# Attention and a two-layer ReLU network in one kernel: from unit 3 on q and k are split for two heads at once, scores run as 64-row float16 matmuls, V is split once per unit, g's low parts go to VectorE, and a unit's first layer-2 block stands later

## The chip, the cores and the metric

The kernel runs on one core of a Trainium2 chip. The metric is the device time of one execution in microseconds (us); less is better.

## The reference, cut

```
scores = scale * np.matmul(q, k.transpose(0, 1, 3, 2))       # q, k, v: batch 4, 8 heads, 768 positions, 64 columns
is_global = pos[None, :] < n_global                          # 8
is_local = (rel >= 0) & (rel < n_local)                      # 96
scores = scores - slopes[:, None, None] * dist[None, :, :]   # -1e9 where neither holds
a = np.exp(scores - max); a = a / (sum + 1e-09)
x = np.matmul(a, v)                                          # as 3072 tokens of 512 columns
h = x @ w_in                                                 # w_in 512 x 2048, float32
g = np.maximum(h, 0.0) + alpha * np.minimum(h, 0.0)
out = g @ w_out                                              # w_out 2048 x 512, float32
```

## The kernel before

The 3072 tokens are cut into 12 units of 256 (three to a batch). A query sees at most 96 keys back and 8 global ones, so a unit needs four 128-key blocks of K and V (three in units 0, 3, 6 and 9, which begin a batch). Each unit goes through attention, head by head (`attend`), and then through the network: 16 blocks of layer 1 (`ff_in`, 12 matmuls of 256 columns into a PSUM tile `h`) and 16 of layer 2 (`ff_out`, for each of two 128-token halves 3 matmuls of 512 columns into an accumulator `o`). float32 accuracy is kept with pairs of float16 numbers: a high part, and a rest that `rest` works out; a product is then the three matmuls high by high, high by low, low by high.

Units 0 to 2 are "plain": their scores and values are float32 matmuls (the scores on 64 rows, `sp<-first` and `sp<-raw`), and their probabilities are transposed on TensorE. From unit 3 on one head goes like this. One DMA brings q and k (each twice, on partitions 0 to 63 and again on 64 to 127) and V as `raw` (464 KB, 368 KB in units 3, 6, 9). ScalarE or VectorE scales q into `q2` and k into `khi` (L343, L344), VectorE writes the rests (L368): q's into the lower 64 partitions of `q2`, k's into `klo`. The scores `sp` are then two 128-row matmuls a window, `q2` by `khi` and `q2` by `klo` (L656). V is split in the same way into `vhi` and `vlo`. VectorE adds the bias and finds the maximum (L662), ScalarE takes the exponential (L667), the result is split into `ps`, a DMA transposes it into `pt`, and 18 or 24 matmuls for two heads make `av` (L733), which VectorE scales into `xn`. After eight heads `xn` is split and transposed by DMA into `xt`, the input of layer 1. Behind layer 1 ScalarE multiplies by alpha, VectorE takes the maximum (`g`, L816), ScalarE makes the high part (L818), and VectorE or GpSimd the low one (L367).

The order on every engine comes from a planner (`Plan`): each operation has a key (its due time in slots of one `ff_in` and one `ff_out`), engines it may run on with a cost each, and buffers; the planner plays the program through and the instructions are then issued in the order that it found. `begin(u)` is the slot at which unit u's attention begins: 22 slots before its first `ff_in`, so that units' attention runs beside the network of the unit before. Numbers of buffers: `sp` 2, `av` 2, `h` 2, `o` 2 in PSUM; `raw` 2, `khi`, `klo`, `q2` 2, `vhi`, `vlo` 3, and 17 buffers `rw` of 4 KB a partition, which hold raw weights early and `g` later. Unit 1's accumulators are, by `ff_out`, one `sp` and one `av` buffer; every other unit uses the two `o`.

## Time and profile before

| | |
|---|---|
| time, median of 3 runs | 657.1 us (656.23 to 658.21) |
| the profiled execution's own time | 655.59 us |
| its span, first to last instruction | 653.8 us |
| TensorE (PE) busy | 624.0 us, 95% |
| VectorE (DVE) busy | 518.0 us, 79% |
| ScalarE (ACT) busy | 406.8 us, 62% |
| GpSimd (POOL) busy | 129.1 us, 20% |

In the rows, an instruction stands as line, engine, operation, out<-in with buffer numbers left out, the shape, and a count; the share of time that an engine sat idle before a group stands behind it with the engine and line that ended it. A matmul's busy time runs to the modelled end of its pipeline, so that matmuls which follow each other overlap; what one costs is read from start to start.

### The profile page before, as it was taken

The page shows a single profiled execution, that of the slowest core. Times are in us where ns is not written, and L with a number is a line of the kernel's source. Part 1 is how long each engine was busy: PE and PEld are TensorE (multiplying, and loading weights), DVE is VectorE, ACT ScalarE, POOL GpSimd, SP SyncE. Part 2 cuts the span into 40 slices and gives each one's busy share as a digit, 9 for nine tenths or more (in the row PEclk, how much of TensorE's full clock was granted, in tenths as well). Part 3 has the DMA queues.
Part 4 walks back from the last instruction along what each step waited for, and adds up shares of the span by engine and source line. Part 5 has one row for each costly group of instructions (what it writes and reads, how often), then busy time and mean ns, then how long its engine had stood idle before and what let it go on. Part 6 is the DMA issues. An engine that isn't in the chain of part 4 may idle for free.

```text
span 653.8 us, 13833 instructions
## 1 busy us (share of the span) xinstructions
PE 624.0 (95%) x4964; PEld 438.0 (67%) x4964; DVE 518.0 (79%) x1497; ACT 406.8 (62%) x1085; POOL 129.1 (20%) x185
## 2 busy tenths in 40 slices
PE   8998998999999999899899999999899999999995
PEld 7785666675666666576567676676576677676663
DVE  6899999868888899877989887877988888874331
ACT  6998866536756666766666665673656666653332
POOL 1003342212222223112222122111222112100000
PEclk9999999999999999999999999999999999999998
DMA  8998311115747546843656647764666646621001
GB/s 307 403 406 330 102 59 60 59 55 152 179 103 172 148 105 129 236 116 92 136 151 139 188 102 126 204 155 63 171 156 124 172 133 125 167 47 38 33 1 39
DMA packets 115807, 92.90 MB, mean 142 GB/s; under 512 B 93968, under 2 KB 93968, under 8 KB 115728
## 3 DMA queue, kind: packets, MB, share of 16 engines
q1 hardware_dynamic: 115728, 91.91, 52.1%
q8 instruction: 41, 0.67, 0.4%
q14 instruction: 38, 0.31, 0.2%
HBM read 63.06 MB, written 6.29 MB: 106 GB/s over the span
## 4 chain that ended last, share of the span: by engine, by line
PE 33%; DVE 30%; DMA 20%; ACT 11%; issue 4%; POOL 1%; SPq 0%; ACTq 0%; DVEq 0%; POOLq 0%
DMA raw<-in_qkv_dram 15%; PE o L835 13%; PE h L795 13%; ACT pr L667 4%; DVE ps L368 4%; DVE g L816 3%; DVE klo L368 3%; PE sp L656 3%; DVE q L368 2%; DVE vlo L368 2%; PE av L733 2%; DMA xt<-xs 2%; DMA vr<-in_v_dram 2%; DVE pr L662 2%; DVE vhi L344 2%
## 5 line engine op out<-in xcount | busy, mean ns | idle before, releaser
L795 PE MATMUL h<-xt,whl 128*128 128x256 f16 x2304 | 281.2, 273 | 1.6 <-DVE g L816 1.2
L795 PEld LDWEIGHTS <-whl 128*128 128x128 f16 x2304 | 224.6, 98 | 63.4 <-issue 3.0
L835 PE MATMUL o<-whl,g 128*128 128x512 f16 x864 | 215.6, 379 | 5.4 <-ACT os L842 5.3
L835 PEld LDWEIGHTS <-g 128*128 128x128 f16 x864 | 82.6, 98 | 71.6 <-issue 8.1
L367 POOL TENSOR_TENSOR g<-g 128x256 f16<-128x256 f32 x88 | 67.9, 773 | 256.5 <-ACT g L818 254.1
L667 ACT ACTIVATE pr<-pr,sm 128x256 f32<-128x256 f32 (+1 forms) x192 | 92.7, 484 | 34.9 <-DVE sm L662 34.5
L343 ACT ACTIVATE g<-h,ak 128x256 f32<-128x256 f32 x167 | 77.9, 467 | 55.2 <-PE h L795 52.6
L816 DVE SCALAR_TENSOR_TENSOR g<-h,g 128x256 f32<-128x256 f32 x192 | 80.0, 418 | 32.4 <-ACT g L343 32.0
L818 ACT CAST g<-g 128x256 f16<-128x256 f32 x144 | 57.1, 399 | 59.0 <-DVE g L816 58.6
L662 DVE CUSTOM_DVE_ANT_0 pr<-sp,D 128x256 f32<-128x256 f32 (+1 forms) x192 | 71.3, 393 | 3.5 <-PE sp L656 2.7
L368 DVE SCALAR_TENSOR_TENSOR ps<-pr,ps 128x512 f16<-128x512 f32 (+1 forms) x72 | 49.0, 680 | 12.9 <-ACT ps L343 12.6
L835 PE MATMUL o<-whl,gh 128*128 128x512 f16 x192 | 57.2, 379 | 0.7 <-ACT gh L818 0.6
L367 POOL TENSOR_TENSOR gl<-g,gh 128x256 f16<-128x256 f32 x32 | 30.2, 945 | 110.2 <-ACT gh L818 99.2
L368 DVE SCALAR_TENSOR_TENSOR klo<-raw,khi 128x416 f16<-128x416 f32 (+1 forms) x72 | 43.6, 605 | 1.8
L835 PE MATMUL o<-whl,gl 128*128 128x512 f16 x96 | 36.5, 380 | 2.4 <-POOL gl L367 2.0
L368 DVE SCALAR_TENSOR_TENSOR q<-raw,q 64x256 f16<-64x256 f32 x72 | 32.8, 455 | 6.8 <-ACT q L343 3.9
L367 DVE TENSOR_TENSOR g<-g 128x256 f16<-128x256 f32 x56 | 23.8, 425 | 16.5 <-ACT g L818 16.3
L656 PE MATMUL sp<-klo,q 128*128 128x256 f16 (+1 forms) x144 | 34.0, 263 | 2.3 <-DVE klo L368 2.3
L667 ACT ACTIVATION_READ_ACCUMULATOR pr<-pr,sm 128x1 f32 x192 | 36.2, 189 | 0.0
L733 PEld LDWEIGHTS <-pt 128*128 128x128 f16 x792 | 28.4, 98 | 11.3 <-DMA pt<-ps 3.5
L368 DVE SCALAR_TENSOR_TENSOR vlo<-raw,vs,vhi 128x256 f16<-128x256 f32 (+1 forms) x72 | 35.8, 517 | 0.1
L656 PE MATMUL sp<-khi,q 128*128 128x256 f16 (+1 forms) x144 | 33.8, 264 | 2.1 <-DVE sm L662 1.3
(122 smaller groups left out, 734.6 us busy)
## 6 DMA issues: line engine op xcount, KB each, us to landing
raw<-in_qkv_dram SPq DMA_DIRECT2D x56, 464.0 KB, 3.9
w<-in_w_dram SPq DMA_DIRECT2D x32, 512.0 KB, 9.0
raw<-in_qkv_dram SPq DMA_DIRECT2D x24, 368.0 KB, 3.4
out_dram<-os SPq DMA_DIRECT2D x24, 256.0 KB, 2.4
vr<-in_v_dram SPq DMA_DIRECT2D x18, 256.0 KB, 4.0
first<-in_first_dram SPq DMA_DIRECT2D x4, 464.0 KB, 5.3
vr<-in_v_dram SPq DMA_DIRECT2D x3, 512.0 KB, 8.4
first<-in_first_dram SPq DMA_DIRECT2D x4, 336.0 KB, 10.1
```

Source lines behind the costliest of these rows:

```text
L343: lambda: nc.scalar.mul(out=out(), in_=src(), mul=by.t if tile_ else by)),
L344: DVE=("DVE", c_dve(n, not psum, tile_), lambda: v.tensor_scalar(out=out(), in0=src(), scalar1=by.t if tile_ else by, scalar2=None, op0=AL ...
L367: return e.tensor_tensor(out=out(), in0=src(), in1=hi(), op=ALU.subtract)
L368: return e.scalar_tensor_tensor(out=out(), in0=src(), scalar=val(), in1=hi(), op0=ALU.mult, op1=ALU.subtract)
L656: nc.tensor.matmul(sp.t[:, pc : pc + n], lhsT=q_()[:, 128 * qb : 128 * qb + 128], rhs=kk()[:, off : off + n], start=j == 0, stop=j == len( ...
L662: op("DVE", key, c_dve(n) + 10, lambda qb=qb, n=n, dc=dc, pc=pc: v.tensor_tensor_reduce(out=pr.t[:, pc : pc + n], in0=sp.t[:, pc : pc + n] ...
L667: op("ACT", key + 1, c_act(n, ptr=1) + 93, lambda qb=qb, n=n, pc=pc: nc.scalar.activation(out=pr.t[:, pc : pc + n], in_=pr.t[:, pc : pc + ...
L733: nc.tensor.matmul(out, lhsT=p_[:, 128 * j : 128 * j + 128], rhs=v_[:, 64 * j : 64 * j + 64], start=m == 0, stop=m == len(ps) - 1)
L795: nc.tensor.matmul(hp.t, lhsT=w.t[:, wi, wc], rhs=x.t[:, NC * xi + c, :], start=n == 0, stop=n == 3 * NC - 1)
L816: op("DVE", key, c_dve(UT), lambda: v.scalar_tensor_tensor(out=g_(), in0=hp.t, scalar=KG, in1=g_(), op0=ALU.mult, op1=ALU.max), r=[hp], w= ...
L818: op("ACT", key, c_act(UT), lambda: nc.scalar.copy(out=gh_(), in_=g_()), r=[rg], w=[rh])
L835: nc.tensor.matmul(o.t, lhsT=g_()[:, tok], rhs=w.t[:, wi, 512:1024], start=f == 0 and n == 0, stop=f == NF - 1 and n == 2)
```

## The change

From unit 3 on, `load_pair` takes the place of the splits of q and k: one DMA brings two heads' q and k, head 2i on partitions 0 to 63 and head 2i+1 on 64 to 127 (344 KB, 272 KB in units 3, 6, 9), one instruction makes the high parts `x16` of all of it and one the rests, and the scores of both heads are issued together: for each window three products, each for the one head and then the other, on 64 rows, into two `sp` buffers. `load_v` loads a unit's V once (512 KB), scales and splits it for all heads in four instructions, and builds the blocks of earlier and global keys `gp` by DMAs of up to 96 partitions from this and the last unit's tiles; the matmuls of `av` read `v16` and `gp`. Unit 2 loads q, k and V in the form of unit 1. g's low parts from unit 3 on name VectorE first instead of GpSimd. `ff_out` of block 0 is due at slot 4.05 behind its `ff_in` instead of 3, the others at 3.05. The V ranges of a batch (`v_range`) are due four slots earlier. The layouts in DRAM are made to match. Lines of the changed kernel are some 28 higher in `ff_in` and `ff_out` (L823, L863), scores stand at L648 and `av` at L761.

```
-BUFS = dict(rw=17, raw=2, q2=2, khi=2, klo=2, vhi=3, vlo=3, pr=2, sm=6, pt=2, ps=2, xn=1, xt=2, g=3, gh=3, gl=3,
+BUFS = dict(rw=17, raw=3, x16=3, pr=2, sm=6, pt=2, ps=2, xn=1, xt=2, g=3, gh=3, gl=3,
...
+            x = buf("rw", f"first{u}_{h}", [P, 1024]) if u < 2 else buf("raw", f"first{u}_{h}", [P, 672])
...
+        v16, gp = {}, {}
+        def load_v(u, key):
+            b, c = divmod(u, 3)
+            raw = buf("rw", f"vraw{u}", [P, 1024])
+            x = v16[u] = buf("rw", f"v16_{u}", [P, 1024])
+            g = gp[u] = buf("rw", f"gp{u}", [P, 1024])
+            view = lambda y: y.t.bitcast(F16).rearrange("p (j s k) -> p j s k", j=2, s=2)
+            op("SP", key, c_dma(P * 4096), lambda: nc.sync.dma_start(
+                out=raw.t.rearrange("p (j k) -> p j k", j=2), in_=a["v"][b, 2 * c : 2 * c + 2].rearrange("j p k -> p j k")),
+               w=[raw])
+            for j in range(2):
+                in_ = lambda j=j: raw.t[:, 512 * j : 512 * j + 512]
+                hi, lo = (lambda j=j: view(x)[:, j, 0]), (lambda j=j: view(x)[:, j, 1])
+                k = key + VS + 0.1 * j
+                mul(k, hi, in_, vs[b], [raw, vs[b]], [(x, (j, 0))], "ACT", 512)
+                rest(k, lo, in_, vs[b], hi, [raw, vs[b], (x, (j, 0))], [(x, (j, 1))], 512)
+            key += VS + 1
+            def move(i, part, to, first, last, src, j, parts):
+                n = last - first
+                op("SP", key + 0.1 * i, c_dma(n * 2048), lambda: nc.sync.dma_start(
+                    out=view(g)[to : to + n, i], in_=view(src)[first:last, j]), r=[(src, p) for p in parts], w=[(g, part)])
+            if c:
+                move(0, "0p", 0, GL, P, v16[u - 1], 1, ((1, 0), (1, 1)))
+                move(0, "0g", LOC, LOC, P, gp[u - 1], 1, ("1g",))
+                move(1, "1g", LOC, LOC, P, gp[u - 1], 1, ("1g",))
+            else:
+                move(1, "1g", LOC, 0, GL, x, 0, ((0, 0), (0, 1)))
+            move(1, "1p", 0, GL, P, x, 0, ((0, 0), (0, 1)))
+        def blocks(u):
+            own = [(v16[u], j, [(v16[u], (j, t)) for t in range(2)]) for j in range(2)]
+            far = [(gp[u], j, [(gp[u], f"{j}p"), (gp[u], f"{j}g")]) for j in range(2)]
+            return [far[0], own[0], far[1], own[1]] if u % 3 else [own[0], far[1], own[1]]
+        pair = {}
+        def load_pair(u, h, key):
+            nk = 416 if u % 3 else 288
+            n = 256 + nk
+            raw = buf("raw", f"raw{u}_{h}", [P, 672])
+            x = buf("x16", f"x16_{u}_{h}", [P, 2, 672], F16)
+            op("SP", key - KP - 4, c_dma(P * 4 * n), lambda: nc.sync.dma_start(
+                out=raw.t[:, :n], in_=a["qk"][u - 1, h // 2, :, :n]), w=[raw])
+            hi, lo = (lambda: x.t[:, 0, :n]), (lambda: x.t[:, 1, :n])
+            mul(key - KP, hi, lambda: raw.t[:, :n], QS, [raw], [(x, 0)], n=n)
+            rest(key - KP, lo, lambda: raw.t[:, :n], QS, hi, [raw, (x, 0)], [(x, 1)], n)
+            if (u, h) == (3, 0):
+                for i in range(H):
+                    op("POOL", key - KP, c_pool(384, 1), lambda i=i: nc.gpsimd.tensor_scalar(
+                        out=Dh[i].t, in0=Dh[i].t, scalar1=QS * QS, scalar2=None, op0=ALU.mult), w=[Dh[i]])
+            sps = [buf("sp", f"sp{u}_{h + i}", [P, 512]) for i in range(2)]
+            for i in range(2):
+                pair[u, h + i] = sps[i]
+            def scores():
+                for qb, off, m, _, pc in windows(u):
+                    for j, (qi, ki) in enumerate(((0, 0), (0, 1), (1, 0))):
+                        for i, sp in enumerate(sps):
+                            rows = slice(64 * i, 64 * i + 64)
+                            nc.tensor.matmul(sp.t[:, pc : pc + m], lhsT=x.t[rows, qi, 128 * qb : 128 * qb + 128],
+                                             rhs=x.t[rows, ki, 256 + off : 256 + off + m], start=j == 0, stop=j == 2)
+            op("PE", key, 3 * 0.426 * (512 if u % 3 else 384) + 300, scores, r=[x], w=sps)
         def attend(u, h, key):
...
-                raw = buf("raw", "raw" + uh, [P, 928])
-                op("SP", kp - 4, c_dma(P * 4 * (256 + nk + nv)), lambda: nc.sync.dma_start(
-                    out=raw.t[:, : 256 + nk + nv], in_=a["qkv"][u, :, h, : 256 + nk + nv]), w=[(raw, 0), (raw, 1)])
...
-                q2 = buf("q2", "q2_" + uh, [P, 256], F16)
-                q_ = lambda: q2.t
-                khi = buf("khi", "khi" + uh, [P, 416], F16)
-                klo = buf("klo", "klo" + uh, [P, 416], F16)
-                kk = lambda: rawt()[:, 256 : 256 + nk]
-                mul(kp, lambda: q2.t, lambda: rawt()[:, :256], QS, [rq], [q2], n=256)
-                mul(kp, lambda: khi.t[:, :nk], kk, QS, [rq], [khi], n=nk)
-                rest(kp, lambda: q2.t[64:, :], lambda: rawt()[64:, :256], QS, lambda: q2.t[64:, :], [rq], [q2], 256)
-                rest(kp, lambda: klo.t[:, :nk], kk, QS, lambda: khi.t[:, :nk], [rq, khi], [klo], nk)
...
-            if not plain:
-                vhi = buf("vhi", "vhi" + uh, [P, 256], F16)
-                vlo = buf("vlo", "vlo" + uh, [P, 256], F16)
-                vv = lambda: vrt()[:, :nv]
...
-                    mul(kp + 3, lambda: vhi.t[:, :nv], vv, vs[b], [rv, vs[b]], [vhi], "DVE", nv)
-                    rest(kp + 3, lambda: vlo.t[:, :nv], vv, vs[b], lambda: vhi.t[:, :nv], [rv, vs[b], vhi], [vlo], nv)
...
+                if h % 2 == 0:
+                    load_pair(u, h, key)
+                sp = pair[u, h]
...
-                    for j, (_, kk) in enumerate(keys):
-                        nc.tensor.matmul(sp.t[:, pc : pc + n], lhsT=q_()[:, 128 * qb : 128 * qb + 128],
-                                         rhs=kk()[:, off : off + n], start=j == 0, stop=j == len(keys) - 1)
-            op("PE", key, cost, scores, r=[q2] + [x for x, _ in keys], w=[sp])
+                    nc.tensor.matmul(sp.t[:, pc : pc + n], lhsT=qk_()[:, 128 * qb : 128 * qb + 128],
+                                     rhs=qk_()[:, 256 + off : 256 + off + n], start=True, stop=True)
+            if plain:
+                op("PE", key, 2 * npr * 0.84, scores, r=[q2], w=[sp])
...
+                vb = blocks(u)
+                def side(j, t):
+                    y, i, _ = vb[j]
+                    return y.t.bitcast(F16)[:, 1024 * i + 512 * t + 64 * h : 1024 * i + 512 * t + 64 * h + 64]
+                prods = lambda: ((pflat(), lambda j: side(j, 0)), (pflat(), lambda j: side(j, 1)),
+                                 (pflat()[:, npr:], lambda j: side(j, 0)))
+                used = [pt] + [x for _, _, y in vb for x in y]
...
-                        nc.tensor.matmul(out, lhsT=p_[:, 128 * j : 128 * j + 128], rhs=v_[:, 64 * j : 64 * j + 64],
+                        nc.tensor.matmul(out, lhsT=p_[:, 128 * j : 128 * j + 128], rhs=v_(j),
...
-            rest(key, gl_, g_, None, gh_, [rg, rh], [rl], UT, "DVE" if u < 2 and f < 2 else "POOL")
+            rest(key, gl_, g_, None, gh_, [rg, rh], [rl], UT, "DVE" if u > 2 or u < 2 and f < 2 else "POOL")
...
+            if u > 2:
+                jobs.append((begin(u) - VL, load_v, (u,)))
...
-                jobs.append((slot(u, f) + (DP if u < 2 else 1.5 if u == 2 else DL), ff_out, (u, f)))
+                jobs.append((slot(u, f) + (DP if u < 2 else 1.5 if u == 2 else DL + (1.05 if f == 0 else 0.05)), ff_out, (u, f)))
```

PE, the scores of unit 7's first two heads. Before: the last matmul of a layer-1 block `h5_10`, the weight load and the two products of head 0 (each stands twice, once a window), then layer 2; head 1 has the same rows later, behind `h5_12`.

```order
L795 MATMUL h5_10_4936<-xt5_4296,whl10_1349 128x256
L656 LDWEIGHTS q2_7_0_4864
L656 MATMUL sp7_0_4954<-khi7_0_4866,q2_7_0_4864 128x256
L656 MATMUL sp7_0_4954<-klo7_0_4894,q2_7_0_4864 128x256
L835 MATMUL o5_1_4593<-whl7_1097,g5_7_4812 128x512
```

Now:

```order
L823 MATMUL h5_10_4692<-xt5_4187,whl10_1356 128x256
L648 LDWEIGHTS x16_7_0_4226
L648 MATMUL sp7_0_4706<-x16_7_0_4226 128x256
L648 MATMUL sp7_1_4708<-x16_7_0_4226 128x256
L863 MATMUL o5_0_4478<-whl7_1089,g5_7_4605 128x512
```

The rows `sp7_0` and `sp7_1` stand six times each, turn about: two blocks of four matmuls have become one of twelve, and the second head's scores stand in the place of the first's.

PE where unit 5's layer 2 takes over the accumulators from unit 4 (`o4_1` with `g4_15` is unit 4's last block, `o5_0` with `g5_0` unit 5's first; one row for each block of 3, 4, 12 or 18 matmuls). Before:

```order
L656 MATMUL sp6_2_4534<-khi6_2_4501,q2_6_2_4499 128x256
L835 MATMUL o4_1_3857<-whl15_1732,g4_15_4398 128x512
L835 MATMUL o5_0_4552<-whl0_543,g5_0_4438 128x512
L656 MATMUL sp6_3_4561<-khi6_3_4527,q2_6_3_4525 128x256
L795 MATMUL h5_3_4570<-xt5_4296,whl3_812 128x256
L835 MATMUL o5_1_4593<-whl0_543,g5_0_4438 128x512
```

Now:

```order
L863 MATMUL o4_0_3754<-whl15_1737,g4_15_4266 128x512
L863 MATMUL o4_1_3772<-whl15_1737,g4_15_4266 128x512
L823 MATMUL h5_3_4413<-xt5_4187,whl3_802 128x256
L761 MATMUL av6_2_4433<-v16_6_4134,pt6_2_4314 128x64
L823 MATMUL h5_4_4458<-xt5_4187,whl4_858 128x256
L863 MATMUL o5_0_4478<-whl0_533,g5_0_4328 128x512
L863 MATMUL o5_0_4478<-whl1_594,g5_1_4356 128x512
```

Between the last block of the old unit and the first of the new stood nothing; now two layer-1 blocks and one of `av` stand there, and blocks 0 and 1 of layer 2 follow each other.

PE where unit 3's attention begins (`o1` is unit 1's accumulators, in an `sp` and an `av` buffer; rows as above, in part). Before, head 0 stood ahead of unit 1's last layer-1 block:

```order
L835 MATMUL o1_0_1010<-whl12_1485,gl1_12_1884 128x512
L656 MATMUL sp3_0_1996<-khi3_0_1976,q2_3_0_1974 128x128
L656 MATMUL sp3_0_1996<-klo3_0_1981,q2_3_0_1974 128x256
L835 MATMUL o1_0_1010<-whl13_1578,gl1_13_1956 128x512
L835 MATMUL o1_0_1010<-whl14_1639,gl1_14_2020 128x512
```

Now:

```order
L863 MATMUL o2_0_2139<-whl1_594,gl2_1_2136 128x512
L863 MATMUL o1_0_1000<-whl15_1737,gl1_15_2092 128x512
L648 MATMUL sp3_0_2179<-x16_3_0_1451 128x128
L648 MATMUL sp3_1_2181<-x16_3_0_1451 128x128
L648 MATMUL sp3_0_2179<-x16_3_0_1451 128x256
L648 MATMUL sp3_1_2181<-x16_3_0_1451 128x256
```

A pair takes both `sp` buffers, so unit 3's first scores stand behind the last block of `o1_0`; its four pairs then follow with some 1.5, 2 and 3.5 blocks of the network between them.

## Rows read from the trace of the kernel before

**Rows 1.** The page's first part: the span, then busy time, share of the span and instructions of each engine.

```profile
span 653.8 us, 13833 instructions
PE 624.0 (95%) x4964; PEld 438.0 (67%) x4964; DVE 518.0 (79%) x1497; ACT 406.8 (62%) x1085; POOL 129.1 (20%) x185
```

**Rows 2.** Busy time by stretch: the stretch in us, its length, then busy us and instructions of PE, PEld (weight loads), DVE, ACT, POOL, the granted clock of PE (1.00 is full speed), the share of the DMA engines and GB/s. 30 to 150 holds the network of units 0 and 1 and the splitting of the weights, 150 to 210 that of unit 2 beside unit 3's attention, 210 to 600 units 3 to 10, the last stretch unit 11 with no attention beside it.

```profile
30.00:150.00 120.00, 114.87 (x802) 82.95 (x803) 109.98 (x264) 84.50 (x205) 31.42 (x27) 1.00 0.45 159
150.00:210.00 60.00, 57.84 (x474) 38.35 (x473) 51.17 (x158) 39.43 (x106) 14.70 (x21) 1.00 0.60 145
210.00:600.00 390.00, 377.81 (x3208) 264.66 (x3206) 319.92 (x933) 242.32 (x664) 79.13 (x123) 1.00 0.57 137
600.00:653.80 53.80, 46.25 (x308) 30.03 (x305) 15.46 (x48) 17.00 (x37) 0.67 (x1) 0.96 0.06 22
```

**Rows 3.** Who waited for whom, 210 to 600 us: the matmuls (PE) and, last row, the weight loads. Columns: us in total, times, the longest.

```profile
PE o L835 <- ACT os L842: 5.3, 7, 2.2
PE av L733 <- DMA pt<-ps: 2.9, 5, 1.2
PE sp L656 <- DVE klo L368: 2.3, 8, 0.5
PE h L795 <- DVE g L816: 1.2, 2, 0.7
...
PEld L656 <- DVE q L368: 2.5, 7, 0.4
```

**Rows 4.** The same view, 140 to 210 us.

```profile
PE sp L656 <- DVE sm L662: 1.3, 2, 0.8
PE o L835 <- ACT gh L818: 0.6, 2, 0.4
...
PEld L835 <- POOL gl L367: 1.7, 3, 0.6
```

**Rows 5.** Instructions in order of time: start us, us, engine, line, operation, out<-in, shape, count, and in brackets the idle time before and what ended it. PE and ACT where unit 5's layer 2 begins.

```profile
261.93 0.81 PE L835 MATMUL o<-whl,g 128*128 128x512 f16 x3
...
264.23 0.67 ACT L842 ACTIVATE os<-o,osc 128x512 f32<-128x512 f32 x1
...
264.95 0.81 PE L835 MATMUL o<-whl,g 128*128 128x512 f16 x3 [2.21 <-ACT os L842]
```

**Rows 6.** PE in order of time: scores of unit 6 (128 and 256 columns), and blocks of both layers.

```profile
311.60 0.22 PE L656 MATMUL sp<-klo,q 128*128 128x128 f16 x1 [0.51 <-DVE klo L368]
311.66 0.27 PE L656 MATMUL sp<-khi,q 128*128 128x256 f16 x1
311.77 0.27 PE L656 MATMUL sp<-klo,q 128*128 128x256 f16 x1
...
313.94 1.47 PE L795 MATMUL h<-xt,whl 128*128 128x256 f16 x12
315.25 1.46 PE L835 MATMUL o<-whl,g 128*128 128x512 f16 x6
316.55 1.47 PE L795 MATMUL h<-xt,whl 128*128 128x256 f16 x12
318.07 0.23 PE L656 MATMUL sp<-khi,q 128*128 128x128 f16 x1
```

**Rows 7.** PE in order of time, unit 1's 64-row float32 scores: one head (21.52) and, later, two heads issued one behind the other on rows 0 to 63 and 64 to 127 (24.45), each with the block that follows.

```profile
21.52 1.13 PE L656 MATMUL sp<-first 64*128 64x256 f32 x4
22.58 0.66 PE L693 MATMUL tp<-ident,pr 128*128 128x128 f32 x4
...
24.45 1.14 PE L656 MATMUL sp<-first 64*128 64x256 f32 x8
25.52 1.09 PE L771 MATMUL xp<-ident,xn 128*128 128x128 f32 x8
```

**Rows 8.** PE in order of time: one such block of unit 2 between blocks of the network.

```profile
108.81 0.71 PE L795 MATMUL h<-xt,whl 128*128 128x256 f16 x5
109.45 1.13 PE L656 MATMUL sp<-raw 64*128 64x256 f32 x4
110.51 0.61 PE L835 MATMUL o<-whl,gh 128*128 128x512 f16 x2
```

**Rows 9.** Groups of equal instructions, shapes apart: count, busy us and mean ns of one, then idle time before them and what ended it.

```profile
L368 DVE SCALAR_TENSOR_TENSOR q<-raw,q 64x256 f16<-64x256 f32 x72 | 32.8, 455 | 6.8 <-ACT q L343 3.9
L368 DVE SCALAR_TENSOR_TENSOR klo<-raw,khi 128x416 f16<-128x416 f32 x48 | 31.9, 665 | 1.2
L368 DVE SCALAR_TENSOR_TENSOR vlo<-raw,vs,vhi 128x256 f16<-128x256 f32 x48 | 26.4, 571 | 0.1
L368 DVE SCALAR_TENSOR_TENSOR ps<-pr,ps 128x512 f16<-128x512 f32 x48 | 33.2, 692 | 12.7 <-ACT ps L343 12.6
L367 DVE TENSOR_TENSOR g<-g 128x256 f16<-128x256 f32 x56 | 23.8, 425 | 16.5 <-ACT g L818 16.3
L367 POOL TENSOR_TENSOR g<-g 128x256 f16<-128x256 f32 x88 | 67.9, 773 | 256.5 <-ACT g L818 254.1
L662 DVE CUSTOM_DVE_ANT_0 pr<-sp,D 128x256 f32<-128x256 f32 x160 | 64.8, 415 | 0.6 <-PE tp L693 0.3
```

**Rows 10.** DMA issues: tile, count, KB each, median us from issue to landing.

```profile
vr<-in_v_dram SPq DMA_DIRECT2D x18, 256.0 KB, 4.0
...
pt<-ps SPq DMA_TRANSPOSE x72, 3.1
```

More of the change, by code (lines that the diff above doesn't have):

```diff
@@ L315 @@
 WLEAD = 8
-VLEAD = 22
+VLEAD = 26.5
+VS = 5
+VL = 4
 WARM = 9
@@ L546, in load_first @@
         def load_first(u, h, key):
[L548 removed]
+            x = buf("rw", f"first{u}_{h}", [P, 1024]) if u < 2 else buf("raw", f"first{u}_{h}", [P, 672])
             nk, n = (672, 672) if u else (544, 928)
             def load():
[L552 removed]
+                nc.sync.dma_start(out=x.t[:, :n], in_=a["qk"][u - 1, h // 2] if u else a["first0"][h // 2])
                 if u == h == 0:
@@ L643, in attend @@
-            sp = buf(idle(u, h, "sp", "h"), "sp" + uh, [P, 512])
+                if u == 2 and h % 2 == 0:
+                    load_first(u, h, key - KP - 4)
+                q2, qk_ = first[u, h]
+                rv, vrt = firstv[u, h]
+                sp = buf(idle(u, h, "sp", "h"), "sp" + uh, [P, 512])
+            else:
+                if h % 2 == 0:
+                    load_pair(u, h, key)
+                sp = pair[u, h]
             pr = buf(idle(u, h, "pr", "stage"), "pr" + uh, [P, 512])
@@ L703, in attend @@
                 ps = buf("ps", "ps" + uh, [P, 2, 512], F16)
-                pt = buf("wf" if PT4 and u > 2 else "pt", "pt" + uh, [P, 2, 512], F16)
+                pt = buf("pt", "pt" + uh, [P, 2, 512], F16)
                 pp = lambda: pr.t[:, :npr]
```

72 lines of the change are left out of this document (15 added, 57 removed).

## Prediction

> **What bounds the kernel now.** I read the page's busy line first [rows 1]: TensorE is busy in 95% of the span, VectorE in 79%. A busy engine need not be the bound, so the table by stretch comes next [rows 2]: from 210 to 600 us TensorE works 377.8 of 390 us, at the granted clock 1.00 (the 2.4 GHz level), VectorE 319.9, ScalarE 242. So TensorE sets the time there, and a change can help in two ways only: fewer start-to-start nanoseconds of matmuls, or shorter waits of TensorE. In the last stretch, without attention beside it, there is nothing to win. From 30 to 150 us TensorE and VectorE are both near full (114.9 and 110.0 of 120), with weights to split, which the change leaves as it is.
>
> The floor of the matmuls, from start to start [rows 6]: a layer-1 block of 12 takes 1.31 us (0.109 each), a layer-2 block of 6 1.30, a score matmul of 256 columns 0.11 and of 128 columns 0.056.
>
> The waits are in the view of who waited for whom [rows 3]. Its idle time begins at a matmul's modelled end. In [rows 5] three matmuls start at 261.93, three times 0.216 later the next could start (262.58), and it starts at 264.95: 2.37 us lost where the row says 2.21. So I add 0.16 a wait. From 210 to 600 us:
> - layer 2's first block, for ScalarE to empty the accumulator (os): 5.3 + 7 x 0.16 = 6.4
> - av, for the transposes pt: 2.9 + 0.8 = 3.7
> - scores, for k's low part: 2.3 + 1.3 = 3.6; for q's, seen at the weight load, 318.07 against 316.55 + 1.31 [rows 6] is 0.21, I take 0.15 for each of 7, 1.0
> - layer 1, for g (a full h): 1.2 + 0.3 = 1.5
>
> Together 16.2 us. From 140 to 210 us [rows 4] the same count gives 1.3 + 0.6 + 0.6 for the matmuls' waits and 1.7 less some 0.2 each for those seen only at the weight loads, with q's about 4 us.
>
> **The change, part by part.**
>
> *Scores on TensorE.* Before: units 4, 5, 7, 8, 10, 11 have 8 heads x 4 matmuls x 0.109 = 3.5 us each, units 3, 6, 9 8 x 2 x (0.056 + 0.109) = 2.6 us; together 28.8 us. After: three products instead of two, each on half the rows. If two heads' matmuls on the two halves run at once, a pair costs 6 x 0.109 = 0.65 or 3 x 0.165 = 0.50 us, for 24 and 12 pairs 21.6 us; if they run one by one, 43.2. The trace decides for the first: one head's block of four 64-row matmuls takes 1.06 us to the next block's start (21.52 to 22.58), two heads' eight take 1.07 (24.45 to 25.52) [rows 7].
>
> But such a block costs something at its edges [rows 8]. From the start of five layer-1 matmuls at 108.81 to the layer-2 block at 110.51 pass 1.70 us; five by 0.109 and four float32 ones by 0.216 are 1.41. So 0.29 us go at each block for entering and leaving. The first weight load in it is a float32 one, longer than the float16 one here; bounds 0.20 and 0.30 us, I take 0.25, for 36 blocks 9.0 us (7.2 to 10.8). Net: 21.6 + 9.0 - 28.8 = +1.8 us (0 to +3.6). The saved matmuls pay for the edges, no more.
>
> The Trainium skill bears on both halves. TensorEngine Tiling (Array Packing), section Overview, gives a contraction of at most 64 rows "up to 2x"; by that alone the scores would give back 7.2 us and the sum below would end at 637. Its section Tiling Modes says that "Mode switching requires drain", without a price; the trace agrees, and prices it at 0.29 us a block.
>
> *Splits.* VectorE loses the rests of q (32.8 us), k (31.9, and those of units 3, 6, 9) and V (26.4, likewise) [rows 9], and scalings. It gains 36 rests of up to 672 columns (0.69 us at 512 columns, 0.665 at 416; 0.7 to 1.07 each: 25 to 39 us), 18 of V at 0.69 (12 us) and 88 low parts of g that were GpSimd's, at 0.425 (37 us): lighter by 10 us or more, with GpSimd's 67.9 us gone. None of this is on the path by itself, since TensorE is the bound. What it buys is that a split is ready in time. In order of issue the split of a pair now stands some 11 us of TensorE work ahead (x16 and raw have three buffers, each for two heads). So of 4.6 us for q and k I count 4.2 as gone.
>
> *Softmax and transposes.* Two heads' scores stand together; av stands, counted over the blocks between in the two orders, 16 us of TensorE work behind the scores instead of 9. The pt transposes take 3.1 us to land [rows 10]. Of 3.7 us I count 2.8 as gone. The price is a burst: four bias steps of 0.415 [rows 9] in a row ahead of g's next step. With VectorE lighter I count 0.8 of the 1.5 us for g as gone.
>
> *First layer-2 block.* Between a unit's last block and the next one's first stood 0 to 2.3 us of TensorE work; now two layer-1 blocks and an av block, 3.8 us from the first half's end. The longest wait was 2.37 us and the others 1.3 or less, so 5.8 of 6.4 us go.
>
> *Unit 3.* Unit 1's accumulator holds an sp buffer, so the first pair stands behind its last block, and the four pairs follow close. VectorE needs 4 x 0.3 to 0.4 us and the reads behind them, about 2 us, before sp is free, and the second pair stands 1.9 us behind the first. The waits of unit 2's g stay: its low parts remain GpSimd's. Bounds -2 and +3; I take +1.0.
>
> *V parts.* TensorE does the same matmuls. The DMAs that build gp are new; landing bounded by 0 and the 4.0 us of the V loads [rows 10], issued some 3 us behind a unit's first scores and needed 16 us behind them: hidden, 9 us to spare. Less DMA traffic is hidden either way (share 0.57 [rows 2]). Unit 2's new loads move the same scores: nothing.
>
> Sum, against the profiled execution's own 655.6: - 4.2 - 2.8 - 0.8 - 5.8 = -13.6, +1.8, +1.0: 644.8. That execution lies 1.5 us under the median of the runs, so 646.3; I say 646.
>
> **The rivals.**
>
> *All waits go and the edges are cheap.* 655.6 - 16.2 - 3 + 0 = 636.4, with the 1.5 638. For it: the waits are short and every cover grows. Against: unit 3's tight start.
>
> *The waits come back.* Bursts of a pair (four bias steps, four exponentials, the 672-column rest on VectorE ahead of g's maximum) make h or g late. If half of the 13.6 returns, 653. Against: layer 2 of a block stands three slots behind its layer 1, and some 6 us of TensorE work between a pair and the block that needs the delayed h.
>
> *The two heads don't overlap in float16.* 43.2 instead of 21.6 us: 644.8 + 21.6 + 1.5 = 668, slower. It decides once a pair's block costs 0.30 us more than forecast (the win of 10.8 us over 36 pairs); one by one it costs 0.60 more. Against it stands [rows 7], in float32.
>
> *V's parts late.* The gp DMAs stand in SP's queue behind V's last rest; should TensorE wait 2 us a unit, 18 us, 664: slower. From 1.2 us a unit the win is gone. Against: the 9 us to spare.
>
> **How the numbers follow.** Forecast (641 to 652) 0.62; all waits gone 0.13; waits back 0.13 (0.10 still faster, 0.03 within); no overlap 0.06; V late 0.06 (0.02 within). About 0.3% (2 us) is what a measurement of this kernel can tell from no change. Faster 0.85, same 0.05, slower 0.10. The range from 637 to 654 takes in the ends of the unknown costs and leaves out the two slow rivals and part of the first.
>
> **What would show it.** Right: per-pair blocks with two starts some 10 ns apart and about 0.65 us long plus 0.2 to 0.3 at the edges; os, klo and q gone from TensorE's waits or under 1.5 us together from 210 to 600 us; GpSimd nearly idle; VectorE under 510 us. Wrong: score matmuls of a pair 0.109 apart one by one; TensorE waiting for gp; new rows of h waiting for g of more than 5 us; or pairs waiting for sp beyond unit 3.

## The result, and the profile after

The kernel after takes 642.1 us (median of four runs, 638.8 to 642.4), the kernel before, beside it, 656.9: ratio 0.976, 95% interval 0.973 to 0.980. A second timing on another chip gave 0.973 (0.970 to 0.975). The forecast was 646 with a range of 637 to 654; faster had 0.85.

The profiled execution took 642.33 us, its span 640.5. The page's first part, as in [rows 1]:

```profile
span 640.5 us, 13718 instructions
PE 620.4 (97%) x5108; PEld 427.5 (67%) x5108; DVE 454.1 (71%) x1319; ACT 390.1 (61%) x1016; POOL 78.1 (12%) x108
```

Busy time by stretch, with the columns of [rows 2]:

```profile
30.00:150.00 120.00, 114.40 (x778) 82.48 (x776) 111.60 (x259) 83.77 (x200) 34.94 (x31) 0.97 0.47 165
150.00:210.00 60.00, 58.80 (x518) 39.04 (x518) 42.77 (x132) 38.07 (x101) 9.52 (x15) 1.00 0.55 107
210.00:600.00 390.00, 387.91 (x3427) 263.95 (x3426) 266.83 (x795) 233.15 (x616) 30.45 (x49) 1.00 0.49 109
```

Who waited for whom on TensorE, 210 to 600 us, is one row where [rows 3] has five:

```profile
PE h L823 <- DVE g L844: 2.0, 2, 1.1
```

From 210 to 600 us TensorE now works 387.9 of 390 us, VectorE 267 instead of 320. The waits for os, pt, klo and q are gone. The row that is left (1.2 us before) is two waits where the attention of units 6 and 9 begins. In the first, at 290 us, VectorE has V's scaling and rest (0.65 and 1.65 us) between g's product with alpha and g's maximum:

```profile
290.20 0.47 DVE L340 TENSOR_SCALAR g<-h,ak 128x256 f32<-128x256 f32 x1
290.59 0.65 DVE L340 TENSOR_SCALAR v<-vraw,vs 128x512 f16<-128x512 f32 x1
291.16 1.65 DVE L364 SCALAR_TENSOR_TENSOR v<-vraw,vs,v 128x512 f16<-128x512 f32 x1
292.73 0.41 DVE L844 SCALAR_TENSOR_TENSOR g<-h,g 128x256 f32<-128x256 f32 x1
```

Where the time went is best told by when the first layer-1 matmul of a unit starts in the two traces. Units 2, 3 and 11 start at 151.8, 205.7 and 600.3 us before, and at 154.3, 207.1 and 586.0 after. So: up to unit 2, +2.5; unit 2 beside unit 3's attention, -1.1; from unit 3's network to unit 11's ("units 3 to 10" below), 394.6 to 378.9, -15.7; the end, +1.0. The sum, -13.3, is the difference of the two executions, 655.6 and 642.3. The stretch from 210 to 600 us above reaches 14 us into unit 11's network in the kernel after, so that the two are compared by units below.

**What the rows before had shown and the prediction had not read.** VectorE and ScalarE each work through a queue in order. In the kernel before both stand for `raw`, a head's q, k and V. This is who waited for whom, 210 to 590 us, kernel before: VectorE and ScalarE, and the DMA queue, whose `raw` loads (L612) wait until the low part of V has been read out of a `raw` buffer:

```profile
DVE q L344 <- DMA raw<-in_qkv_dram: 16.0, 18, 1.5
DVE khi L344 <- DMA raw<-in_qkv_dram: 3.7, 8, 0.7
...
ACT q L343 <- DMA raw<-in_qkv_dram: 21.6, 19, 3.0
ACT khi L343 <- DMA raw<-in_qkv_dram: 11.6, 14, 1.6
...
SPq L612 <- DVE vlo L368: 33.1, 23, 7.2
```

Together 52.9 us of two engines. Of the 2.21 us wait for os in [rows 5] the timeline before tells more: V's low parts end at 259.2, two `raw` loads are issued at 260.05, ScalarE and VectorE wait until 263.91 for them, and the eviction os stands behind the split of q in ScalarE's queue.

```profile
258.32 0.87 DVE L368 SCALAR_TENSOR_TENSOR vlo<-raw,vs,vhi 128x256 f16<-128x256 f32 x2
260.05 1.00 SPq L612 DMA_DIRECT2D raw<-in_qkv_dram  x2
263.91 0.42 ACT L343 ACTIVATE q<-raw 128x256 f16<-128x256 f32 x1 [1.28 <-DMA raw<-in_qkv_dram]
263.91 0.38 DVE L344 TENSOR_SCALAR khi<-raw 128x416 f16<-128x416 f32 x1 [0.59 <-DMA raw<-in_qkv_dram]
```

So the row "waited for os" names, in this longest of its seven waits, the last link of a chain that begins with a full `raw` buffer; the other six were not followed back. The change gives `raw` three buffers of two heads each, without V. In the trace after, neither engine waits for `raw` in that stretch (VectorE once, 1.3 us, for `vraw`, the load of V).

### The profile page after: what moved, and what is told of

It reads as the page before. It is cut to its first block, busy times and chain, and to the rows that moved or that the text cites. A ratio compares the mean times of both kernels' runs of the same rounds, so it can differ in the third digit from the quotient of the medians.

```text
span 640.5 us, 13718 instructions
## 1 busy us (share of the span) xinstructions
PE 620.4 (97%) x5108; PEld 427.5 (67%) x5108; DVE 454.1 (71%) x1319; ACT 390.1 (61%) x1016; POOL 78.1 (12%) x108
## 4 chain that ended last, share of the span: by engine, by line
PE 78%; DVE 10%; DMA 4%; ACT 3%; issue 3%; POOL 1%; SPq 0%; DVEq 0%; ACTq 0%; POOLq 0%
PE h L823 34%; PE o L863 33%; PE av L761 4%; PE sp L648 4%; PE sp L682 2%; DMA first<-in_qk_dram 2%; DVE wf L532 1%; DVE wb L529 1%; DVE whl L364 1%; ACT pr L693 1%; DVE g L844 1%; POOL gl L363 1%; DVE v L364 1%; PE tp L719 1%; DMA gp<-v 1%
## 5 line engine op out<-in xcount | busy, mean ns | idle before, releaser
L823 PE MATMUL h<-xt,whl 128*128 128x256 f16 x2304 | 284.2, 274 | 3.3 <-DVE g L844 2.9
L823 PEld LDWEIGHTS <-whl 128*128 128x128 f16 x2304 | 223.7, 98 | 60.7 <-issue 7.5
L863 PE MATMUL o<-whl,g 128*128 128x512 f16 x864 | 208.3, 379 | 0.0
L863 PEld LDWEIGHTS <-g 128*128 128x128 f16 x864 | 82.1, 98 | 79.3 <-ACT g L339 5.3
L363 DVE TENSOR_TENSOR g<-g 128x256 f16<-128x256 f32 x132 | 55.7, 422 | 34.2 <-ACT g L846 34.1
L688 DVE CUSTOM_DVE_ANT_0 pr<-sp,D 128x256 f32<-128x256 f32 (+1 forms) x192 | 67.4, 397 | 2.5 <-PE sp L682 1.7
L863 PE MATMUL o<-whl,gh 128*128 128x512 f16 x192 | 57.4, 381 | 0.1
L706 POOL TENSOR_TENSOR fin<-fin,sm 128x4 f32<-128x4 f32 x36 | 11.2, 311 | 267.4 <-ACT pr L693 267.4
L863 PE MATMUL o<-whl,gl 128*128 128x512 f16 x96 | 36.7, 382 | 2.1 <-POOL gl L363 2.0
L761 PEld LDWEIGHTS <-pt 128*128 128x128 f16 x792 | 28.1, 98 | 6.6 <-DMA pt<-ps 0.8
L339 ACT ACTIVATE ps<-pr 128x512 f16<-128x512 f32 (+1 forms) x52 | 30.6, 588 | 3.1 <-DMA pt<-ps 2.3
L364 DVE SCALAR_TENSOR_TENSOR x<-raw,x 128x672 f16<-128x672 f32 (+1 forms) x36 | 30.3, 840 | 0.0
L863 PEld LDWEIGHTS <-gh 128*128 128x128 f16 x192 | 18.1, 99 | 15.7 <-issue 1.5
L648 PE MATMUL sp<-x 64*128 64x256 f16 (+1 forms) x432 | 28.1, 262 | 0.2 <-DVE sm L688 0.2
L761 PE MATMUL av<-v,pt 128*128 128x64 f16 x432 | 27.1, 193 | 0.7 <-DMA pt<-ps 0.7
```

The costliest lines, as they stand in the source:

```text
L339: lambda: nc.scalar.mul(out=out(), in_=src(), mul=by.t if tile_ else by)),
L363: return e.tensor_tensor(out=out(), in0=src(), in1=hi(), op=ALU.subtract)
L364: return e.scalar_tensor_tensor(out=out(), in0=src(), scalar=val(), in1=hi(), op0=ALU.mult, op1=ALU.subtract)
L648: nc.tensor.matmul(sp.t[:, pc : pc + m], lhsT=x.t[rows, qi, 128 * qb : 128 * qb + 128], rhs=x.t[rows, ki, 256 + off : 256 + off + m], star ...
L688: op("DVE", key, c_dve(n) + 10, lambda qb=qb, n=n, dc=dc, pc=pc: v.tensor_tensor_reduce(out=pr.t[:, pc : pc + n], in0=sp.t[:, pc : pc + n] ...
L761: nc.tensor.matmul(out, lhsT=p_[:, 128 * j : 128 * j + 128], rhs=v_(j), start=m == 0, stop=m == len(ps) - 1)
```

## The experiments

Each was timed beside the kernel before on one chip; ratios are to that, and medians of different sessions were taken on different chips. "Units 3 to 10" is the stretch defined above, from each run's trace; "raw" is what VectorE and ScalarE together waited for `raw` from 210 to 590 us. The planner works out the order anew for each edit, so that other operations change their place or engine too. The two executions of the kernel after differ by 0.1 us in units 3 to 10.

| kernel | median us | ratio, 95% interval | units 3 to 10 | raw |
|---|---|---|---|---|
| before | 656.9 to 661.0 | 1 | 394.6 | 52.9 |
| before, later first block | 659.1 | 1.002 (0.998 to 1.005) | 397.0 | 49.0 |
| before, g's low parts on VectorE | 652.1 | 0.992 (0.988 to 0.996) | 388.0 | 34.9 |
| before, three raw buffers | 647.5 | 0.984 (0.981 to 0.987) | 382.0 | 5.3 |
| before, V once per unit | 640.9 | 0.972 (0.969 to 0.974) | 380.6 | 0 |
| after | 642.3 | 0.973 (0.970 to 0.975) | 378.8 | 0 |
| after, first block at its old place | 638.0 | 0.969 (0.965 to 0.972) | 377.2 | 0 |
| after, g's low parts on GpSimd | 640.3 | 0.972 (0.969 to 0.976) | 378.9 | 0 |
| after, both undone | 640.7 | 0.970 (0.967 to 0.973) | 378.8 | 0 |
| after, same rows | 661.3 | 1.005 (1.003 to 1.007) | 397.0 | 0 |
| after, head by head | 642.1 | 0.978 (0.973 to 0.982) | 379.1 | 0 |
| after, early g (blocks 2, 3) | 636.1 | 0.963 (0.961 to 0.965) | 377.1 | 0 |
| after, early g (blocks 0 to 5) | 637.1 | 0.969 (0.966 to 0.971) | 377.6 | 0 |

### The small parts, each alone

**The later first layer-2 block, on the kernel before.**

```diff
-slot(u, f) + (DP if u < 2 else 1.5 if u == 2 else DL), ff_out
+slot(u, f) + (DP if u < 2 else 1.5 if u == 2 else DL + (1.05 if f == 0 else 0.05)), ff_out
```

> The kernel before, with only the order of the layer-2 blocks changed (first block of a unit one place later, the others as good as unmoved). Theory (TensorE bounds the kernel, each wait that goes is a gain of its own size): the waits for the evictions os, about 6 us in all, go; 650 to 652 us, ratio 0.990 to 0.993. Rival (the splits on VectorE pace the units, a wait removed in one place comes back in another): the waits on q, klo and pt grow by what os loses; 655 to 658 us, ratio within 0.3% of 1.

Ratio 1.002 (0.998 to 1.005): no gain. TensorE's waits, 210 to 590 us:

```profile
PE av L733 <- DMA pt<-ps: 7.8, 6, 2.3
PE h L795 <- DVE g L816: 4.2, 4, 1.6
PE sp L656 <- DVE klo L368: 2.0, 8, 0.3
PE sp L656 <- DVE q L368: 1.2, 1, 1.2
```

os is gone, as the theory said, but pt and g grew from 2.9 and 1.2 to 7.8 and 4.2: 15.2 us against 11.7 before in these rows. The rival holds. Whatever holds up the two queues makes TensorE wait for the next thing that stands in them.

**The same edit undone in the kernel after.**

```diff
-DL + (1.05 if f == 0 else 0.05)
+DL
```

> The kernel after, with the first layer-2 block of a unit back at its old place. Theory (the later block is what removed the os waits): they come back at 0.5 to 0.6 us a unit, 645 to 648 us. Rival (the lighter VectorE and ScalarE evict in time anyway, the move was not needed): 641 to 643 us, no os row over 0.2 us in all between 210 and 590.

0.969 (0.965 to 0.972), and no wait of TensorE at all is left from 210 to 590 us: the rival again. In the kernel after, the later block took away none of the waits. In the traces it costs a little: units 3 to 10 take 377.2 instead of 378.9 us without it, and the network of unit 11 ends 45.9 us behind its start instead of 46.6. By the medians this is not settled: undone together with the next part, beside the kernel after on one chip, the intervals overlap.

**g's low parts back on GpSimd, in the kernel after.**

```diff
-rest(key, gl_, ..., "DVE" if u > 2 or u < 2 and f < 2 else "POOL")
+rest(key, gl_, ..., "DVE" if u < 2 and f < 2 else "POOL")
```

> The kernel after, with the low parts of g back on GpSimd from unit 3 on. Theory (VectorE at 71% has room either way; the buffers of h are given free by the maximum on VectorE, which queues behind less when the low parts are away): h waits at the starts of units 6 and 9 shrink from 2.3 us to under 1, total 641 to 643 us, within 0.3%. Rival (the move to VectorE earned something: GpSimd's low parts of 0.7 us and more, beside a busy VectorE, come late for the layer-2 blocks): waits on gl or g of 1 to 4 us between 210 and 590, 643 to 647 us.

0.972: as the kernel after. The two waits for g stay (2.0 us); that they would shrink was wrong. The move to VectorE earned nothing beside the rest of the change.

**g's low parts on VectorE, in the kernel before** (the opposite edit).

> The kernel before, with only the low parts of g on VectorE from unit 3 on. Theory (before, VectorE's splits are the late producers; 132 more instructions of 0.42 us, 56 us, go ahead of them in its queue): waits on q, klo, g and pt grow, 660 to 670 us. Rival (VectorE has room, and GpSimd's slow low parts are what made g late): the h waits of 1.5 us shrink, 655 to 657 us.

0.992 (0.988 to 0.996): 0.8% faster, where the theory said slower. Two things were off. The planner had already put 38 of these low parts on VectorE between 210 and 590 us, so it gained 80, not all; and some of VectorE's other instructions became shorter. Groups of VectorE, 210 to 590 us, kernel before, and then this one:

```profile
L368 DVE SCALAR_TENSOR_TENSOR klo<-raw,khi 128x416 f16<-128x416 f32 (+1 forms) x59 | 36.3, 615 | 1.5
L368 DVE SCALAR_TENSOR_TENSOR vlo<-raw,vs,vhi 128x256 f16<-128x256 f32 (+1 forms) x59 | 30.3, 535 | 0.1
```

```profile
L368 DVE SCALAR_TENSOR_TENSOR klo<-raw,khi 128x416 f16<-128x416 f32 (+1 forms) x60 | 33.6, 560 | 1.4
L368 DVE SCALAR_TENSOR_TENSOR vlo<-raw,vs,vhi 128x256 f16<-128x256 f32 (+1 forms) x61 | 27.2, 461 | 0.2
```

615 to 560 ns and 535 to 461 ns, with GpSimd's busy time in the whole span down from 129 to 79 us. This is no matter of shapes: the 128x416 instructions alone go from 665 to 598 ns, the 128x256 ones from 582 to 479, though the 128x512 ones for `ps` stay at 692 and 688. So VectorE is faster beside a GpSimd with less to do. The waits for `raw` fall from 52.9 to 34.9 us; that they fall because V's low parts end sooner fits the chain above, but no run parts it from the new order. The Trainium skill, SBUF — State Buffer, section "Who interferes with whom", states a rule for it: a VectorE instruction with two inputs in SBUF contends with a GpSimd instruction that reads SBUF. The trace agrees for `klo` and `vlo`, and does not show it for `ps`.

**Both small parts undone in the kernel after, beside the kernel after itself** (the first edit below is none, the second is the two undone edits above together).

> The kernel after, unchanged, timed beside the three below on one chip, since the undone later block gave 0.9686 on another chip and the whole change 0.9761. If the later first layer-2 block really costs something, this is 0.974 to 0.978 and the kernel with the splits only lies 0.4 to 0.8% under it; if the difference was between chips, both lie within 0.3% of each other.

> The kernel after with both small parts undone: the first layer-2 block at its old place and the low parts of g on GpSimd again; the q, k split for two heads and V split once per unit remain. Theory (the lighter splits alone end the waits, the two small parts are not needed beside them): 637 to 641 us, ratio 0.968 to 0.975, waits of TensorE between 210 and 590 under 3 us in all. Rival (the parts add up as forecast, 5.8 for the later block and 0.8 for g): 645 to 649 us, os rows back.

0.973 and 0.970 with overlapping intervals: no difference that these runs can tell (the forecast sum would have had 645 or more). The splits alone bring the whole gain.

### Which of the splits, and why

**V split once per unit, on the kernel before.** A head's load and splits keep only q and k; V is loaded and split once per unit, and the edge blocks are moved, as in the change (`load_v`, `blocks`, VLEAD 26.5).

```diff
-    in_=a["qkv"][u, :, h, : 256 + nk + nv]), w=[(raw, 0), (raw, 1)])
+    in_=a["qkv"][u, :, h, : 256 + nk]), w=[(raw, 0)])
...
-    mul(kp + 3, lambda: vhi.t[:, :nv], vv, vs[b], ...)
-    rest(kp + 3, lambda: vlo.t[:, :nv], vv, vs[b], ...)
```

> The kernel before with V split once per unit and nothing else of the change (q, k still split head by head, 128-row scores). It takes some 59 low parts of 0.535 us and 41 high parts of 0.425 us off VectorE and puts 14 low parts of about 0.9 us there: some 30 us of VectorE less. Theory (late splits are one common cause of the waits on q, klo, pt, h and os): waits between 210 and 600 fall from 16 us to 4 to 8, 645 to 651 us, ratio 0.982 to 0.991. Rival (as with the later block alone, waits only move): 655 to 659 us.

0.972 (0.969 to 0.974), better than the theory's 0.982: this part alone is worth as much as the whole change. Both splits together, in the same session (0.970, 0.967 to 0.973), are no faster that these runs can tell: what the split for two heads adds to it is not shown to be more than nothing. TensorE's waits, 210 to 590 us:

```profile
PE h L830 <- DVE g L851: 1.4, 2, 0.9
PE av L768 <- DMA pt<-ps: 0.4, 1, 0.4
PE o L870 <- ACT os L877: 0.3, 1, 0.3
```

It does three things at once, though: VectorE has less to do (516.6 to 482.4 us in the first 640), a `raw` buffer is read out earlier, and a head's load shrinks from 464 to 336 KB. The next run parts the buffer from the work.

**Three raw buffers, on the kernel before.**

```diff
-BUFS = dict(rw=17, raw=2, q2=2, ...
+BUFS = dict(rw=17, raw=3, q2=2, ...
```

> The kernel before with three buffers instead of two for a head's raw q, k and V, and nothing else. It separates the two things that splitting V once per unit did: less work for VectorE, and raw buffers that come free and are filled sooner (in the kernel before VectorE stands 20 us between 210 and 590 waiting for raw at the splits of q and k; with V apart, none). Theory A (VectorE's work is the cause): 655 to 660 us, within 0.4% of the kernel before, the waits of TensorE only moved. Theory B (the raw transfers come late and hold up VectorE's queue): VectorE's idle time before raw falls under 5 us, 646 to 652 us, ratio 0.980 to 0.990.

0.984 (0.981 to 0.987): theory B. VectorE's and ScalarE's waits for `raw`, 210 to 590 us, and then TensorE's waits:

```profile
DVE q L344 <- DMA raw<-in_qkv_dram: 2.0, 2, 1.4
...
ACT q L343 <- DMA raw<-in_qkv_dram: 2.7, 4, 1.0
...
ACT khi L343 <- DMA raw<-in_qkv_dram: 0.6, 1, 0.6
```

```profile
PE av L733 <- DMA pt<-ps: 2.1, 4, 0.6
PE h L795 <- DVE g L816: 0.7, 1, 0.7
PE sp L656 <- DVE klo L368: 0.3, 1, 0.3
```

One number, with all the work of the kernel before, takes 12.6 us out of units 3 to 10, where the whole change takes 15.7; os is gone without any block moved, and klo nearly; pt keeps 2.1 of its 2.9 us. The DMA queue still waits as long for V's low parts (`SPq L612 <- DVE vlo` 35.7 us), but now for a buffer that is needed one head later.

VectorE's work is not quite the same, though: the planner gave ScalarE some of the scalings. These are the rows of units 3 to 10 (columns as in [rows 2]) in the kernels before, before with the later block, before with g's low parts on VectorE, with three raw buffers, and with V once per unit:

```profile
205.70:600.31 394.61, 382.42 (x3245) 267.84 (x3242) 324.44 (x943) 243.42 (x667) 79.80 (x124) 1.00 0.57 136
205.87:602.89 397.02, 381.40 (x3242) 267.61 (x3239) 319.80 (x934) 248.99 (x682) 83.05 (x119) 1.00 0.59 135
208.98:596.99 388.01, 380.86 (x3245) 267.69 (x3242) 329.30 (x1004) 248.14 (x679) 29.47 (x52) 1.00 0.59 139
208.94:590.97 382.03, 378.71 (x3245) 268.14 (x3242) 311.65 (x892) 262.34 (x717) 85.56 (x122) 1.00 0.60 140
205.92:586.54 380.62, 378.43 (x3245) 268.10 (x3242) 289.22 (x815) 254.79 (x705) 80.38 (x116) 1.00 0.61 139
```

VectorE's busy time, 324.4, 319.8, 329.3, 311.7 and 289.2 us, does not order the five lengths: more of it went with a shorter stretch (388.0), less with a longer one (397.0). The waits for `raw`, 52.9, 49.0, 34.9, 5.3 and 0 us, order them but for the first two, 2.4 us apart.

What the profiled execution lacks against V once per unit, 5.7 us, lies for 3.0 ahead of that stretch: unit 3's network starts at 208.9 us here and at 205.9 there. A third buffer also moves the planner's order in the first 120 us, where TensorE now waits 1.6 us at 57 for a weight split on ScalarE and 2.8 at 114 for an xn; why the order fell out so was not studied.

### The scores

**Both heads on the same 64 rows, in the kernel after.**

```diff
-rows = slice(64 * i, 64 * i + 64)
+rows = slice(0, 64)
```

> The kernel after, where both heads of a pair read the same 64 rows (the odd head computes with the even head's q and k), so that nothing can overlap on TensorE. Theory (TensorE is the bound and the overlap of two row halves pays for the 64-row blocks): a pair block grows from about 0.65 us to 1.25 at c not 0 and from 0.5 to 0.95 at c = 0; 24 x 0.6 + 12 x 0.45 = 19.8 us longer, 658 to 664 us. Rival (TensorE has slack at the scores, other engines set the end): under 5 us longer.

The odd heads' own scores are left out here. 661.3 us, 19.2 above the head-by-head kernel of the same session, which runs as the kernel after does. A pair's block between blocks of layer 1, first in the kernel after, then here (TensorE in order of time; the count merges the block's twelve):

```profile
223.36 0.83 PE L648 MATMUL sp<-x 64*128 64x256 f16 x12
224.12 1.04 PE L863 MATMUL o<-whl,g 128*128 128x512 f16 x4
```

```profile
212.81 1.48 PE L648 MATMUL sp<-x 64*128 64x256 f16 x12
214.22 0.50 PE L823 MATMUL h<-xt,whl 128*128 128x256 f16 x3
```

0.76 and 1.41 us to the next block's start: 0.65 more. 24 such pairs, and 12 shorter ones (units 3, 6, 9) by an estimate of 3 x 0.165 = 0.495 us, come to 21.5 us; all but some two of them reach the end. TensorE is the bound, and the overlap of the two row halves is what makes 64-row scores affordable.

**Head by head, in the kernel after.**

```diff
-for j, (qi, ki) in enumerate(((0, 0), (0, 1), (1, 0))):
-    for i, sp in enumerate(sps):
+for i, sp in enumerate(sps):
+    for j, (qi, ki) in enumerate(((0, 0), (0, 1), (1, 0))):
```

> The kernel after with the matmuls of a pair's block issued head by head (three of the even head, then three of the odd one, per window) instead of in turn; the same work and result. Theory (only neighbours in TensorE's queue on different row halves overlap): one start of three pairs overlaps, the block takes 0.22 us less than with the same rows at most, 14 to 19 us longer than the kernel after, 655 to 661 us. Rival (the engine looks further ahead and overlaps them anyway): within 1 us a unit of the kernel after, 640 to 646 us.

642.1 us, and the block takes 0.77 us as when issued in turn:

```profile
210.90 0.84 PE L648 MATMUL sp<-x 64*128 64x256 f16 x12
211.67 0.50 PE L823 MATMUL h<-xt,whl 128*128 128x256 f16 x3
```

The theory fell: the twelve still start in six pairs 10 ns apart (210.898 and 210.908, 211.018 and 211.028, ...; issued in turn they are 3 ns apart, 223.357 and 223.360), though three of one head stand ahead of three of the other in the queue. On the same rows matmuls start 0.109 us apart in the run above, so a pair must be one matmul of each head: the second head's first starts ahead of the first head's second. The Trainium skill, TensorE: Matmul & The Clock Gate, section "The mechanism" under Part 3, calls the matmuls' starts strictly in program order; on two row halves this run shows otherwise.

### A version that beats both

Two stands of TensorE remain ahead of unit 2's network: 2.0 us at 60 for a low part of g on GpSimd that took 4.30 us, and 2.7 us at 111 for an xn on VectorE. The first is in the kernel before as well. GpSimd, then TensorE, kernel after, and the same in the kernel before:

```profile
55.40 4.30 POOL L363 TENSOR_TENSOR gl<-g,gh 128x256 f16<-128x256 f32 x1 [1.78 <-ACT gh L846]
59.75 0.39 PE L863 MATMUL o<-whl,gl 128*128 128x512 f16 x1 [1.99 <-POOL gl L363]
```

```profile
55.87 4.30 POOL L367 TENSOR_TENSOR gl<-g,gh 128x256 f16<-128x256 f32 x1 [1.78 <-ACT gh L818]
60.22 0.39 PE L835 MATMUL o<-whl,gl 128*128 128x512 f16 x1 [1.98 <-POOL gl L367]
```

**Low parts of blocks 2 and 3 in units 0 and 1 on VectorE first, the first layer-2 block at its old place.**

```diff
-"DVE" if u > 2 or u < 2 and f < 2 else "POOL"
+"DVE" if u > 2 or u < 2 and f < 4 else "POOL"
```

> The kernel after with the first layer-2 block at its old place, and in units 0 and 1 the low parts of g of blocks 2 and 3 on VectorE too. Theory (the low part that took 4.3 us on GpSimd at 55 us was shut out by VectorE's run of instructions with two inputs in SBUF, and TensorE's 2.1 us wait for it let the granted clock fall): no wait over 0.6 us between 52 and 70, granted clock 1.00 in 58 to 70, 2 to 4 us under the splits-only kernel, 634 to 638 us. Rival (VectorE has no pause there and only passes the lateness on): the same wait a few us later for another tile, 638 to 641 us.

0.963 (0.961 to 0.965), 636.1 us, against 642.3 for the kernel after on the same chip: 1% less than the change, and the best of all. But not for the reason given. The planner, free to choose, still gave the low part to GpSimd: TensorE stands 2.0 us for it at 60, and the granted clock falls behind that. What changed is the rest of the order: the wait for xn at 111 is 1.9 us instead of 2.5 to 2.7 with no clock fall after it, and no wait of a matmul is left from 210 to 590 us. How much of this is due to the first block's old place alone is not told: that kernel had 0.969 (0.965 to 0.972) on another chip.

**Blocks 0 to 5 on VectorE and nowhere else**, to take the choice away ("only" leaves GpSimd out); the first layer-2 block at its old place here too.

```diff
-"DVE" if u > 2 or u < 2 and f < 2 else "POOL"
+"only" if u < 2 and f < 6 else "DVE" if u > 2 else "POOL"
```

> The kernel after with the first layer-2 block at its old place and, in units 0 and 1, the low parts of g of blocks 0 to 5 on VectorE and nowhere else (in the run before, the planner still gave most of them to GpSimd, and the 4.3 us one at 55 us stayed). Theory (GpSimd shut out by VectorE's back-to-back instructions with two inputs in SBUF is what makes TensorE wait 2.1 us at 60 us): no wait over 1 us between 50 and 70, granted clock 1.00 in 58 to 70; 2 to 3.5 us off the 0.963 of the run before, ratio 0.957 to 0.961. Rival (VectorE has no time to spare there: the low parts push the weight splits back): a wait of 1 us or more on whl or g between 50 and 70, ratio 0.961 to 0.967.

0.969, 637.1 us. Unit 3 starts at 202.5 us, 2.4 earlier than in the run above, and the granted clock is 1.00 from 58 to 120 us; but the rival's waits came too: 0.8 us for a weight split on ScalarE, 0.9 for one on VectorE, 1.1 for g between 54 and 61. That TensorE's 2.0 us stand goes when VectorE does these low parts is shown; that VectorE was what held up the 4.30 us one on GpSimd is not, nor that the exchange pays.

## Why the prediction came out right, and where it did not

**TensorE as the bound**: right. It is at 99.5% between 210 and 600 us, and 21.5 us added to the scores lengthen the kernel by 19. Of the signs of being right, one failed: GpSimd is not nearly idle, it works 30.5 of those 390 us. VectorE became lighter by 64 us (518.0 to 454.1), where "10 us or more" was counted.

**Scores, +1.8**: the mechanism was right, the size off. Twelve matmuls of 256 columns take 0.654 us and the next block starts 0.76 behind the first: 0.10 to leave, and as much to enter (seven layer-1 matmuls from 282.43 take 7 x 0.109 = 0.76, the pair starts at 283.29). 0.20 us a block, the lower bound, and not 0.25: 21.6 + 7.2 - 28.8 = 0.

**Waits, -13.6**: in all 13.9 (16.2 to 2.0 and twice 0.16). The size is right, but the step that shared it out among the edits failed. It took each row of [rows 3] as a wait of its own, with a price and an edit that ends it. For the most part they were one: the queues of VectorE and ScalarE stood for `raw`, and with a third `raw` buffer alone os is gone, klo falls from 2.3 to 0.3 and g from 1.2 to 0.7.
- *os, -5.8, by the later block*: the row went, but the gain is not the later block's. Alone it ends the row and the waits come up elsewhere (1.002); undone, nothing comes back. That the term had the right size is luck.
- *q and klo, -4.2*: gone, but neither VectorE's smaller load nor the pair's split early in the order was needed for it: three buffers on the kernel before leave 0.3 of 2.3 us for klo, and with V apart two buffers leave none. Which of the two does it in the kernel after, no run parts. That `x16` and `raw` have three buffers was counted as cover for TensorE's order only.
- *pt, -2.8*: 3.7 gone. With the buffer alone 2.1 of 2.9 us in the row stay, with V once per unit 0.4; here VectorE's work does seem to matter, but no run parts the two.
- *g, -0.8*: wrong, +0.8: 1.5 us became 2.3, in two places where V is split.

**Unit 3, +1.0**: the sign was wrong. The stretch became 1.1 us shorter. The waits from 140 to 210 us fell from about 4 to about 2 us, and scores waiting for an `sp` buffer, the reason given, from 1.3 to 0.2.

**V's parts hidden**: right; no wait for gp.

**Not in the sum**: +2.5 us up to unit 2. In the profiled execution the granted clock fell behind both early waits, to a mean of 0.86 from 58 to 70 us and 0.83 from 110 to 120, which the kernel before has at 1.00 in its own, behind the same wait at 60. The rows of the two falls, kernel after:

```profile
61.00:64.00 3.00, 3.00 (x15) 1.95 (x14) 3.00 (x8) 1.17 (x4) 0.00 (x0) 0.54 0.88 304
111.40:114.90 3.50, 3.50 (x17) 2.40 (x17) 3.37 (x5) 1.59 (x4) 0.99 (x1) 0.52 0.12 15
```

They cost 3.0 x 0.46 + 3.5 x 0.48 = 3.1 us of work. The repeated execution has the second fall and not the first, and there unit 2 starts at 152.9 us, 1.2 behind the kernel before instead of 2.5.

Against the forecast, by stretches: units 3 to 10 -15.7 where -11.8 was forecast (-13.6 + 1.8), unit 2 beside unit 3's attention -1.1 where +1.0 was, and +2.5 and +1.0 at the two ends where nothing was (0.6 of the +1.0 is the later first block, 46.6 instead of 45.9 us for unit 11's network). That is the 2.5 us by which the execution lies under 644.8. Counted from start to start, TensorE's waits in units 3 to 10 come to 17.3 us before and 2.6 after, so they gave 1.1 us more than forecast; the rest of the -15.7 is the scores (-0.5 in that stretch) and a few layer-2 matmuls that moved out of it (-0.4), but for 0.1. That the sum was near does not show that its terms were: the falls of the clock, which it did not have, brought the time nearer to it.

## What to carry to other kernels

When several engines wait in turn for products of the same two queues, look at what those queues themselves wait for before pricing each wait: here 53 us of VectorE and ScalarE stood for a load whose buffer was held by its last reader, and the bound engine's view showed only the 12 us at the chain's end, under four names, of which one more buffer nearly ended two (os, klo) and left most of a third (pt). A buffer that carries parts with different last readers is free only with the last of them; try one more buffer first, since that is one number (1.6% here), or load the late part by itself (2.8%). An edit that removes one of several waits with one cause can be worth nothing alone. And a change of several parts is worth taking apart: here one of them gave all of the gain that can be told.
